# Thresholded attention and a low-rank mixer on one core: new figures and ranks for the planner that orders the kernel, and the last output block on two queues

## The chip, the cores and the metric

The kernel runs on one core of a Trainium2 chip. The metric is the device time of one execution in microseconds; the median of ten executions stands for the kernel. The profile is one further execution, taken apart by the hardware profiler, with its own time. Engines are named as in the profile: PE is TensorE (matmuls; PEld its weight loads), DVE is VectorE, ACT is ScalarE, POOL is GpSimd, SP is SyncE, which here only issues DMAs.

## What is computed

Eight batches, eight heads, 576 rows, head size 64; all inputs and the output are float32.

```python
def _attn_ref(q, k, v, tau):
    scores = scale * np.matmul(q, k.transpose(0, 1, 3, 2))      # scale = 1/8
    thresh = np.max(scores, axis=-1, keepdims=True) - tau
    scores = np.where(scores >= thresh, scores, -1000000000.0)
    scores = scores - np.max(scores, axis=-1, keepdims=True)
    attn = np.exp(scores)
    attn = attn / (np.sum(attn, axis=-1, keepdims=True) + 1e-09)
    return np.matmul(attn, v)

def _moe_ref(x, U, V, w_ch1, w_ch2):          # x: heads side by side, 8 x 576 x 512
    h = x.transpose(0, 2, 1) @ U @ V          # rank 32 over the 576 rows
    u = x + h.transpose(0, 2, 1)
    ch = np.maximum(u @ w_ch1, 0.0) @ w_ch2   # 512 -> 2048 -> 512
    return u + ch
```

So there is attention that keeps only scores within tau of the row's maximum, then a low-rank mix along the rows, then a two-layer mixer along the columns.

## The kernel before, in words

**Attention.** Heads are taken in pairs, 32 pairs (p = 0 to 31), four to a batch. q and k of a pair are loaded by POOL's queue (line 329), turned on PE (383, 396), and copied to SBUF by ACT (389, 402); v is loaded by SP (349) and split into a high and a low bfloat16 part (411, 415). A *score step* is one tile of 128 rows for both heads: 16 float32 matmuls (449). Two pairs share their last half tiles, so two pairs have nine steps and the whole kernel has 144. For each head DVE scales the scores and takes the minimum (462), ACT makes the threshold (475) and the exponential (482), and DVE selects and sums (489). The selected weights are turned by a DMA transpose on SP for both heads at once (502), or, for some tiles of the first pairs, on PE (509) with a copy by ACT (519). A *product* (568 to 591) multiplies one group of turned tiles with v; there are three groups to a pair. For the first four pairs its matmuls are on line 586, later on 582. The sum of the two parts and the division by the row sums (619, 623, 630, or 607 for the first four pairs) write x, of which there are three buffers, batch b using b modulo 3.

**Low rank and mixer.** A pair's columns go through U and V (643, 649, 658), are added (665), narrowed (672), turned on PE (680) and copied (686) into uT. When the four pairs of a batch are through, its mixer can start: 16 `up` tasks of four matmuls each (750) with a ReLU on ACT (740), for odd batches four `rest` tasks (766) for the 64 last rows of two batches together, and then `down`: four blocks of 128 rows, in odd batches a fifth block i = 4 (the last rows of two batches), each block in four quarters of four matmuls (783) into one bank. Each block ends with a sum on DVE (`finish`, 794) and two DMAs on SP (805 and 806, or twice 809). The weights W1 and W2 come in eight loads each by POOL's queue (839, 842), tied to score steps by the lists `W1_AT` and `W2_AT`; `ups` wait for all of W1, `downs` for all of W2. The ReLU outputs of even and of odd batches have one half each of one buffer, so the mixer of a batch starts after that of the batch two before.

**The planner.** The order of instructions on each engine is not written by hand. The class `Order` (66 to 193) takes tasks with an engine, an estimated cost, what they depend on and how many of four PSUM banks they need, runs them through a model of the machine before anything is issued, and emits the instructions in the order that comes out. Each engine then works through its own instructions in that order, and waits on the chip by the buffers that they use. In the model:

- of an engine's tasks that can start within `PATIENCE[engine]` of the earliest, the one of lowest rank is taken; the rank is the time at which it became ready plus an offset from the table `OFF` (three values by name: for the first four pairs, the middle, and the last four pairs);
- `up`, `rest` and `down` have a due step instead (`when`, from `DUE[b]`). Once as many score steps are placed, such a task goes ahead of all others; before, it is taken only if nothing else can start as early;
- a DMA costs its queue `cost`, starts 0.6 later, shares the DMA engines with the other kind of queue (`SHARE`), and is counted as landed `LANDING` later, one value for POOL's queue and one for the others;
- where PE would be idle for longer than 0.45, it is given matmuls on zeros, called fillers (293).

All of `DUE`, `OFF`, `PATIENCE`, `LANDING`, `BOTH` (the cost of issuing one transpose of both heads) and the lists of loads are figures of this planner. What they change is the order in which instructions are issued.

Of the kernel before, what the change touches and what calls it, by code (L numbers as in the profile page):

```python
# [8 lines left out]
P = 128  # L9
# [6 lines left out]
B, H, S, D = 8, 8, 576, 64  # L16
# [4 lines left out]
HB = 64  # L21
# [1 line left out]
NPAIR = H // 2  # L23
NP = B * NPAIR
SOFT = 4
BOTH = 1.9
EARLY = 8


W1_AT = (5, 7, 9, 11, 13, 15, 17, 19)  # L30
W2_AT = (21, 22, 24, 25, 26, 27, 29, 30)

DUE = (30, 48, 99, 104, 159, 168, 132, 156)

# [9 lines left out]
PE, VEC, SCA, POOL, SP = range(5)  # L46
# [19 lines left out]
class Order:  # L66


    SIGNAL = (0.25, 0.18, 0.15, 0.2, 0.1)
    PATIENCE = (0, 0.2, 0.1, 0.55, 0)  # L70


    BEGIN = (1.2, 4.5, 0.7, 1.3, 0.7)
    LANES = 8
    SHARE = (0.8, 0.2)
    LANDING = (2.3, 1.8)
    SWITCH = {"quadrants": 0.145, None: 0.095}
    PARTS = {"S": "quadrants"}


    OFF = {
        "copy_main": (37, 15, -1), "copy_rest": (-1, -8, -1), "copy_tt": (-23, -22, -3),
        "copy_u": (-22, -16, -2), "copy_u4": (0, 21.25, 0), "copy_w": (39.75, -1, -1),
        "down": (0, 0, 0), "exponential": (21, 43, -10.5), "finish": (-2, -4, -1),
        "first": (-300, 0, 0), "high": (3, -26, -32), "inverse": (-19, -21, 31.5),
        "join": (-22, -6, -4.25), "load": (16, 20, 2), "low": (0, 0, 0),
        "low_part": (-22, -19.5, -40), "low_rank": (-20, -28, -3), "make": (10.75, -2, -2),
        "narrow": (-24, 15, -1), "narrow_u": (-21, 20.25, -1), "narrow_u4": (1, 9, 1),
        "norm": (-24, 2, -4), "product": (-21, 6, -2), "relu": (-2, -11, -2), "rest": (0, 0, 0),
        "scores": (-26, -8, -9), "select": (4.75, 49.25, 29.5), "send": (2, 2, 2),  # L90
        "spread": (-23, -7.25, -3), "spread4": (-1, 15, -1), "spread_v": (16, 5, 5),
        "sum_u": (-21.5, -11, -1.5), "sum_u4": (1, 1, 1), "sums": (0, -1, -1),
        "threshold": (-27, -6, -13), "turn4": (-1, -1, -1), "turn_main": (-2, -1, -4),
        "turn_pe": (-25, 13, -1), "turn_rest": (-3, -2, -2), "turn_u": (-23, -6, -3),
        "turn_w": (-20, 0, 0), "up": (0, 0, 0), "values": (20, 20, 20), "weigh": (-23, -4, -8),
        "weights": (3, 5, 5),
    }

    def __init__(self, nbanks, filler):
# [97 lines left out]
def kernel(  # L197
# [12 lines left out]
    nc = tc.nc  # L210
# [87 lines left out]
    done = {}  # L298

    def got(*key):  # L300
        return done.get(key)
# [126 lines left out]
    def score_tasks(p, i):  # L428
# [51 lines left out]
        for x in range(2):  # L480
            def exponential(_, x=x, e_sb=e_ring[tiles[0] % NS], s_sb=s_ring[tiles[0] % NS]):
                nc.scalar.activation(out=e_sb, in_=s_sb, func=ACT.Exp, bias=m[:, x:x + 1],  # L482
                                     scale=-1.0)

            ex = add(SCA, 0.73, exponential, [mins[x], got("w", tiles[0] - NS)])

            def select(_, x=x, w_sb=w_ring[n % (NW // 2)][:, x, :], e_sb=e_ring[tiles[0] % NS],
                       s_sb=s_ring[tiles[0] % NS]):
                nc.vector.scalar_tensor_tensor(  # L489
                    out=w_sb[:, 0:S], in0=s_sb, scalar=thr_[:, x:x + 1], in1=e_sb,  # L490
                    op0=ALU.is_le, op1=ALU.mult, accum_out=pr.den[:, i, x:x + 1])

            sel = done["w", tiles[0]] = add(
                VEC, 0.77, select, [ex, thr, got("wT", tiles[0] - NW), got("rec", p - 4),
                              got("den4", p - 3)])


            both = not (p < EARLY and 1 <= i < 4)

            def turn_w(_, xs=slice(0 if both else x, x + 1)):  # L500
                to = pr.wT[:, xs, :, i * P:(i + 1) * P] if i < 4 else wT4[:, xs, :, HB:HB + P]
                nc.sync.dma_start_transpose(
                    to.rearrange("p x k r -> p (x k) r"),
                    w_ring[n % (NW // 2)][:, xs, :].rearrange("p x c -> p (x c)"))

            def turn_pe(t, w_sb=w_ring[n % (NW // 2)][:, x, :]):
                ps = bank[t.got[0]][:, 0:320].bitcast(BF16)
                for kt in range(NT):
                    nc.tensor.transpose(ps[:, kt * P:(kt + 1) * P],
                                        w_sb[:, kt * P:(kt + 1) * P], identb)  # L510

            free = [got("AV", p - 2, c) for c in range(2)] if i < 4 else \
                [got("AV", a, 2) for a in (p - 2, p - 1)]
            if i < 4 and (x == 1 and p < EARLY and i >= 1 or p == NPAIR - 1 and i == 3):
                t = done["wT", tiles[0]] = add(PE, 0.28, turn_pe, [sel] + free, banks=1,
                                               kind="wT")

                def copy_w(_, x=x, t=t):
                    nc.scalar.copy(
                        out=pr.wT[:, x, :, i * P:(i + 1) * P],  # L520
                        in_=bank[t.got[0]][:, 0:320].bitcast(BF16).rearrange(
                            "p (k r) -> p k r", k=NT))

                t = add(SCA, 0.68, copy_w, [t], frees=[t])
            elif both and not x:
                t = None
                first_sel = sel
            elif both:
                t = done["wT", tiles[0]] = done["wT", tiles[0] - 1] = add(
                    SP, BOTH, turn_w, [first_sel, sel] + free, dma=2.2)  # L530
            else:
                t = done["wT", tiles[0]] = add(SP, 1.28, turn_w, [sel] + free, dma=1.1)
            if t:
                done.setdefault(("wTs", p, i // 2), []).append(t)
                if i == 4:
                    done.setdefault(("wTs", p + 1, 2), []).append(t)
            tiles[0] += 1
            done.setdefault(("den", p), []).append(sel)
# [9 lines left out]
    def value_tasks(p):  # L548
# [16 lines left out]
        for g, tiles_ in enumerate(((0, 1), (2, 3), (4,))):  # L565
            n = len(tiles_)

            def product(t, tiles_=tiles_):
# [19 lines left out]

            av = done["AV", p, g] = add(
                PE, (0.64 if soft else 0.56) * n, product,  # L590
                done["wTs", p, g] + [done["vlo", p], got("AV", p - 1, g)], banks=1, kind="AV")

            def rows(g=g):
                if g < 2:
# [136 lines left out]
    def mixer_tasks(b):  # L731
# [15 lines left out]
        for ft in range(16):  # L747
            def up(t, ft=ft):
                for dt in range(4):
                    nc.tensor.matmul(bank[t.got[0]], W1b[:, dt, ft * P:(ft + 1) * P],  # L750
                                     bt.uT[:, dt, :], start=(dt == 0), stop=(dt == 3))

            t = add(PE, 0.862, up, uT + weights1 + done.get(("o", b - 2), []), banks=1, kind="p1",
                    when=due + 38.75 * ft / 16)
            done["p1", b].append(t)
            lo = 640 * bt.odd
            relus.append(relu_task(t, slice(ft, ft + 1), lo, lo + 512))
        if bt.odd:

            done["p1r", b] = []  # L760
            for g in range(4):
                def rest(t, g=g):
                    for n in range(4):
                        ft = 4 * g + n
                        for dt in range(4):
                            nc.tensor.matmul(bank[t.got[0]][:, n * P:(n + 1) * P],  # L766
                                             W1b[:, dt, ft * P:(ft + 1) * P], bt.uT4[:, dt, :],
                                             start=(dt == 0), stop=(dt == 3))

                t = add(PE, 0.9, rest, [done["uT4", b], got("o4", b - 2)] + weights1, banks=1,  # L770
                        kind="p1", when=due + -11.75 + 9.75 * g)
                done["p1r", b].append(t)
                relus4.append(relu_task(t, slice(4 * g, 4 * g + 4), 512, 640))

        done["o", b] = []
        for i in range(NT if bt.odd else 4):
            halves = []
            for g in range(4):
                def down(t, i=i, g=g, halves=halves):
                    ch = bank[(halves[0] if g else t).got[0]]  # L780
                    lo = 512 if i == 4 else i * P + 640 * bt.odd
                    for ft in range(4 * g, 4 * g + 4):
                        nc.tensor.matmul(ch, R2[:, ft, lo:lo + P], W2b[:, ft, :],  # L783
                                         start=(ft == 0), stop=(ft == 15))

                when = due + 124 if i == 4 and b < B - 1 else due + 20.5 + 0.25 * (i + g / 4) / 4
                halves.append(add(PE, 0.865, down, (relus4 if i == 4 else relus) + weights2 + halves,
                                  banks=int(not g), kind="ch", when=when))

            o = o_ring[done.setdefault("os", 0) % 3]  # L790
            done["os"] += 1
# [11 lines left out]
            def send(_, i=i, o=o):  # L803
# [1 line left out]
                    nc.sync.dma_start(ov[b, :, i, :], o[0:HB, :])  # L805
                    nc.sync.dma_start(ov[b, :, 5 + i, :], o[HB:P, :])
                else:
                    for e in (bt.even, bt):
                        nc.sync.dma_start(ov[e.b, :, 4, :], o[e.h4, :])

            outs.append(add(SP, 1.2, send, [t], dma=0.9, ndma=2))
            outs.pop(0)
# [100 lines left out]
```

## Time and profile before

| what | us |
|---|---|
| median of ten executions | 623.88 |
| lowest and highest of the ten | 623.18, 633.45 |
| the profiled execution | 634.22 |
| its span, first to last instruction | 632.4 |
| PE busy, of it fillers | 607.2, 20.3 |
| DVE busy | 521.6 |
| ACT busy | 479.4 |
| POOL busy | 285.5 |

The profiled execution is one at the upper end of the ten, so its stages can't be read as those of the median without a correction. The busy time of PE is that of matmuls whose ends are modelled and that overlap; gaps between groups are a better sign of loss than its share. The four groups that use most of PE are the score steps (179.1 us), `down` (133.3), `up` (120.0) and the products of line 582 (90.2).

On DVE the select takes 845 ns and the scaling with the minimum 751 ns for one head's tile, each followed by some 82 ns for reading the sum; two heads make a step, so a step occupies DVE for about 3.5 us. A transpose (502) is issued by SP in 1.35 us and lands 4.0 us after its issue in the median; an output block of 64 rows (128 KB) lands after 2.5 us; loads of q and k take 3.9 to 4.7 us, a part of W1 8.8.

### The profile page before, as it was taken

The page shows a single profiled execution, that of the slowest core. Times are in us where ns is not written, and L with a number is a line of the kernel's source. Part 1 is how long each engine was busy: PE and PEld are TensorE (multiplying, and loading weights), DVE is VectorE, ACT ScalarE, POOL GpSimd, SP SyncE. Part 2 cuts the span into 40 slices and gives each one's busy share as a digit, 9 for nine tenths or more (in the row PEclk, how much of TensorE's full clock was granted, in tenths as well). Part 3 has the DMA queues.
Part 4 walks back from the last instruction along what each step waited for, and adds up shares of the span by engine and source line. Part 5 has one row for each costly group of instructions (what it writes and reads, how often), then busy time and mean ns, then how long its engine had stood idle before and what let it go on. Part 6 is the DMA issues. An engine that isn't in the chain of part 4 may idle for free.

```text
span 632.4 us, 16829 instructions
## 1 busy us (share of the span) xinstructions
PE 607.2 (96%) x6286; PEld 355.5 (56%) x6374; DVE 521.6 (82%) x1406; ACT 479.4 (76%) x983; POOL 285.5 (45%) x396
## 2 busy tenths in 40 slices
PE   8979689999999999999999999999999999999996
PEld 3545356566565555555565555555665546555543
DVE  5988599789988899989988999989989898993202
ACT  5767488997888867997788977798787877894440
POOL 8964245745544345546555454445555513121000
PEclk9998799999999999999999999999999999999999
DMA  7999989985887799889997798989997785553303
GB/s 159 161 133 149 125 131 159 173 128 132 170 133 144 116 167 173 156 134 165 156 153 150 130 162 161 154 140 155 153 161 160 147 134 108 110 96 68 67 1 83
DMA packets 205105, 86.27 MB, mean 136 GB/s; under 512 B 183136, under 2 KB 195376, under 8 KB 205024
## 3 DMA queue, kind: packets, MB, share of 16 engines
q1 hardware_dynamic: 190096, 62.23, 61.7%
q0 software_dynamic: 14048, 22.76, 19.6%
q8 instruction: 50, 0.82, 0.6%
q10 hardware_dynamic: 880, 0.21, 0.2%
q14 instruction: 31, 0.25, 0.1%
HBM read 36.86 MB, written 9.44 MB: 73 GB/s over the span
## 4 chain that ended last, share of the span: by engine, by line
PE 84%; DVE 6%; DMA 5%; issue 3%; ACT 1%; SPq 1%; DVEq 0%; ACTq 0%
PE scores L449 23%; PE bank L783 20%; PE bank L750 16%; PE bank L582 12%; DMA wT_ring<-w_ring 4%; PE bank L383 4%; DVE w_ring L489 2%; DVE s_sb L462 2%; PE bank L766 2%; PE bank L643 1%; PE bank L658 1%; PE bank L680 1%; PE bank L396 1%; DMA vraw_ring<-in_v_dram 1%; PE bank L586 1%
## 5 line engine op out<-in xcount | busy, mean ns | idle before, releaser
L489 DVE SCALAR_TENSOR_TENSOR w_ring<-s_sb,thr,e_sb 128x576 bf16<-128x576 f32 x288 | 238.1, 845 | 11.1 <-ACT thr L475 5.1
L462 DVE TENSOR_SCALAR_CACHE_REDUCE s_sb<-scores 128x576 f32<-128x576 f32 x288 | 207.9, 751 | 40.8 <-PE scores L449 37.6
L482 ACT ACTIVATE e_sb<-s_sb,m 128x576 bf16<-128x576 f32 x288 | 217.3, 770 | 30.2 <-DVE s_sb L462 28.9
L449 PE MATMUL scores<-qkT 64*64 64x288 f32 x2304 | 179.1, 419 | 0.8 <-DVE s_sb L462 0.7
L783 PE MATMUL bank<-W2b,R 128*128 128x512 bf16 x541 | 133.3, 380 | 2.4 <-issue 0.6
L630 POOL TENSOR_TENSOR x<-x,rec 128x256 f32<-128x256 f32 (+1 forms) x84 | 58.9, 702 | 169.3 <-DVE x L623 108.2
L750 PE MATMUL bank<-uT,W1b 128*128 128x512 bf16 x470 | 120.0, 380 | 2.5 <-issue 0.5
L449 PEld LDWEIGHTS scores<-qkT 64*64 64x64 f32 x2304 | 78.3, 133 | 73.9 <-issue 19.6
L740 ACT ACTIVATE R<-bank 128x512 bf16<-128x512 f32 x144 | 84.5, 594 | 22.3 <-PE bank L750 14.5
L329 POOL DMA_DIRECT2D qkraw<-in_q_dram x125 | 82.0, 661 | 38.6 <-PE bank L383 32.6
L415 POOL TENSOR_TENSOR vh<-vraw_ring,vh 128x640 bf16<-128x640 f32 x32 | 50.2, 1569 | 78.5 <-ACT vh L411 68.7
L783 PEld LDWEIGHTS <-R 128*128 128x128 bf16 x576 | 53.3, 98 | 56.3 <-issue 5.7
L329 POOL DMA_DIRECT2D qkraw<-in_k_dram x125 | 81.2, 657 | 6.7 <-DMA qkraw<-in_q_dram 3.9
L750 PEld LDWEIGHTS <-W1b 128*128 128x128 bf16 x512 | 46.0, 98 | 52.1 <-issue 10.2
L582 PEld LDWEIGHTS <-wT_ring 128*128 128x128 bf16 x1120 | 64.8, 98 | 12.6 <-issue 8.8
L582 PE MATMUL bank<-vh,wT_ring 128*128 128x128 bf16 x1120 | 71.7, 220 | 0.0
L794 DVE TENSOR_TENSOR o<-bank,x 128x512 f32<-128x512 f32 x36 | 24.4, 682 | 39.7 <-PE bank L783 36.7
L475 ACT ACTIVATE thr<-m,tau_t 128x2 f32<-128x2 f32 x144 | 42.2, 293 | 4.3 <-DVE s_sb L462 3.8
L389 ACT COPY qkT<-bank 128x512 f32<-128x512 f32 x64 | 35.5, 585 | 9.4 <-PE bank L383 9.1
L623 DVE TENSOR_TENSOR x<-bank,x 128x256 f32<-128x256 f32 (+1 forms) x84 | 30.7, 374 | 8.0 <-ACT x L619 7.3
L383 PE MATMUL bank<-ident,qkraw 128*128 128x128 f32 x256 | 35.0, 275 | 2.2 <-DMA qkraw<-in_q_dram 1.5
L619 ACT COPY x<-bank 128x256 f32<-128x256 f32 (+1 forms) x84 | 26.7, 330 | 10.5 <-PE bank L582 9.9
(70 smaller groups left out, 503.1 us busy)
## 6 DMA issues: line engine op xcount, KB each, us to landing
out_dram<-o SPq DMA_DIRECT2D x72, 128.0 KB, 2.5
vraw_ring<-in_v_dram SPq DMA_DIRECT2D x32, 160.0 KB, 3.9
qkraw<-in_k_dram POOLq DMA_DIRECT2D x63, 80.0 KB, 4.7
qkraw<-in_q_dram POOLq DMA_DIRECT2D x62, 80.0 KB, 3.9
vraw_ring<-in_v_dram SPq DMA_DIRECT2D x32, 128.0 KB, 4.2
qkraw<-in_q_dram POOLq DMA_DIRECT2D x63, 64.0 KB, 4.0
qkraw<-in_k_dram POOLq DMA_DIRECT2D x62, 64.0 KB, 4.6
W1b<-in_moe_w_ch_dram POOLq DMA_DIRECT2D x8, 256.0 KB, 8.8
```

The lines of the kernel that those rows point to most:

```text
L329: queue.dma_start(pr.qkraw[part, to, j, :], src[:, j, of, :])
L383: nc.tensor.transpose(bank[t.got[0]][:, i * P:(i + 1) * P], pr.qkraw[:, t0 + i, :, :], ident)
L415: nc.gpsimd.tensor_tensor(out=pr.vh[:, :, :, 1, :], in0=pr.vraw.rearrange("p j t d -> p t j d"), in1=pr.vh[:, :, :, 0, :], op=ALU.subtract)
L449: nc.tensor.matmul(pair_bank[j][part, c, 0:HC], a.tT[hs, 0, rows], a.tT[hs, 1, cs], start=True, stop=True)
L462: nc.vector.tensor_scalar(out=s_sb.rearrange("p (a c) -> p a c", a=2), in0=pair_bank[x][:, :, 0:HC], scalar1=-scale, scalar2=None, op0=ALU ...
L482: nc.scalar.activation(out=e_sb, in_=s_sb, func=ACT.Exp, bias=m[:, x:x + 1], scale=-1.0)
L489: nc.vector.scalar_tensor_tensor(out=w_sb[:, 0:S], in0=s_sb, scalar=thr_[:, x:x + 1], in1=e_sb, op0=ALU.is_le, op1=ALU.mult, accum_out=pr. ...
L582: nc.tensor.matmul(av[:, 2 * a + j, :], w, pr.vh[:, kt, j, :, :], start=first, stop=last_)
L630: nc.gpsimd.tensor_tensor(out=x, in0=x, in1=over_sum(part), op=ALU.mult)
L740: nc.scalar.activation(out=R2[:, fts, lo:hi], in_=bank[t.got[0]].rearrange("p (f c) -> p f c", c=hi - lo), func=ACT.Relu)
L750: nc.tensor.matmul(bank[t.got[0]], W1b[:, dt, ft * P:(ft + 1) * P], bt.uT[:, dt, :], start=(dt == 0), stop=(dt == 3))
L783: nc.tensor.matmul(ch, R2[:, ft, lo:lo + P], W2b[:, ft, :], start=(ft == 0), stop=(ft == 15))
```

## The change

1. `BOTH` goes; a transpose of both heads is counted at 1.4 of issue. `LANDING` becomes (2.0, 1.4) from (2.3, 1.8), `PATIENCE` of POOL and SP rises to 0.9 and 1.35 from 0.55 and 0.
2. `W1_AT`, `W2_AT`, `DUE` and some 30 of the offsets in `OFF` have new values, and the formulas of `when` new constants.
3. A product depends, in the planner, also on `opens`: the tasks after which the buffers of x are free. Before, only the first task that writes x depended on them.
4. The first quarter of a `down` block depends on the first quarter of the block made before it.
5. The block i = 4 sends its two halves for named batches, and for the last batch the second half goes by ACT's queue.

```diff
-W1_AT = (5, 7, 9, 11, 13, 15, 17, 19)
-W2_AT = (21, 22, 24, 25, 26, 27, 29, 30)
-
-DUE = (30, 48, 99, 104, 159, 168, 132, 156)
+W1_AT = (1, 4, 6, 9, 11, 14, 16, 19)
+W2_AT = (20, 21, 23, 24, 25, 26, 28, 29)
+
+DUE = (30, 48, 66, 87, 163, 120, 127, 156)
...
-    PATIENCE = (0, 0.2, 0.1, 0.55, 0)
+    PATIENCE = (0, 0.2, 0.1, 0.9, 1.35)
...
-    LANDING = (2.3, 1.8)
+    LANDING = (2.0, 1.4)
...
-        "copy_main": (37, 15, -1), "copy_rest": (-1, -8, -1), "copy_tt": (-23, -22, -3),
+        "copy_main": (37, 30, -1), "copy_rest": (-1, -8, -1), "copy_tt": (-26, -59, -3),
...
-        "norm": (-24, 2, -4), "product": (-21, 6, -2), "relu": (-2, -11, -2), "rest": (0, 0, 0),
-        "scores": (-26, -8, -9), "select": (4.75, 49.25, 29.5), "send": (2, 2, 2),
+        "norm": (-24, -1, -4), "product": (-21, 20, 8), "relu": (-2, -45, -2), "rest": (0, 0, 0),
+        "scores": (-26, -69.5, -9), "select": (4.75, 49.25, 0.75), "send": (2, 2, 2),
...
-        "threshold": (-27, -6, -13), "turn4": (-1, -1, -1), "turn_main": (-2, -1, -4),
-        "turn_pe": (-25, 13, -1), "turn_rest": (-3, -2, -2), "turn_u": (-23, -6, -3),
+        "threshold": (-27, -6, -29.5), "turn4": (-1, -1, -1), "turn_main": (-2, -37.75, -4),
+        "turn_pe": (-25, 19.75, -1), "turn_rest": (-3, -38, -5), "turn_u": (-50, -6, -3),
...
-                    SP, BOTH, turn_w, [first_sel, sel] + free, dma=2.2)
+                    SP, 1.4, turn_w, [first_sel, sel] + free, dma=2.2)
...
-                done["wTs", p, g] + [done["vlo", p], got("AV", p - 1, g)], banks=1, kind="AV")
+                done["wTs", p, g] + [done["vlo", p], got("AV", p - 1, g)] + opens, banks=1, kind="AV")
...
-                    when=due + 38.75 * ft / 16)
+                    when=due + 35.75 * ft / 16)
...
-                        kind="p1", when=due + -11.75 + 9.75 * g)
+                        kind="p1", when=due + 3.5 + 10.25 * g)
...
-                when = due + 124 if i == 4 and b < B - 1 else due + 20.5 + 0.25 * (i + g / 4) / 4
-                halves.append(add(PE, 0.865, down, (relus4 if i == 4 else relus) + weights2 + halves,
-                                  banks=int(not g), kind="ch", when=when))
+                when = due + 134.5 if i == 4 and b < B - 1 else due + 46.5 + 13.25 * (i + g / 4) / 4
+                halves.append(add(PE, 0.865, down, (relus4 if i == 4 else relus) + weights2 + (
+                    halves or [got("down")]), banks=int(not g), kind="ch", when=when))
+            done["down"] = halves[0]
...
-                    for e in (bt.even, bt):
-                        nc.sync.dma_start(ov[e.b, :, 4, :], o[e.h4, :])
+
+                    nc.sync.dma_start(ov[b - 1, :, 4, :], o[0:HB, :])
+                    last = nc.scalar if b == B - 1 else nc.sync
+                    last.dma_start(ov[b, :, 4, :], o[HB:P, :])
```

More of the change, by code (lines that the diff above doesn't have):

```diff
@@ L25 @@
 SOFT = 4
-BOTH = 1.9
 EARLY = 8
-W1_AT = (5, 7, 9, 11, 13, 15, 17, 19)
-W2_AT = (21, 22, 24, 25, 26, 27, 29, 30)
-DUE = (30, 48, 99, 104, 159, 168, 132, 156)
+W1_AT = (1, 4, 6, 9, 11, 14, 16, 19)
+W2_AT = (20, 21, 23, 24, 25, 26, 28, 29)
+DUE = (30, 48, 66, 87, 163, 120, 127, 156)
 PE, VEC, SCA, POOL, SP = range(5)
@@ L81 @@
     OFF = {
-        "copy_main": (37, 15, -1), "copy_rest": (-1, -8, -1), "copy_tt": (-23, -22, -3),
[L83 to L87, printed above, removed]
@@ L88 @@
-        "narrow": (-24, 15, -1), "narrow_u": (-21, 20.25, -1), "narrow_u4": (1, 9, 1),
-        "norm": (-24, 2, -4), "product": (-21, 6, -2), "relu": (-2, -11, -2), "rest": (0, 0, 0),
-        "scores": (-26, -8, -9), "select": (4.75, 49.25, 29.5), "send": (2, 2, 2),
-        "spread": (-23, -7.25, -3), "spread4": (-1, 15, -1), "spread_v": (16, 5, 5),
-        "sum_u": (-21.5, -11, -1.5), "sum_u4": (1, 1, 1), "sums": (0, -1, -1),
-        "threshold": (-27, -6, -13), "turn4": (-1, -1, -1), "turn_main": (-2, -1, -4),
@@ L94 @@
-        "turn_pe": (-25, 13, -1), "turn_rest": (-3, -2, -2), "turn_u": (-23, -6, -3),
-        "turn_w": (-20, 0, 0), "up": (0, 0, 0), "values": (20, 20, 20), "weigh": (-23, -4, -8),
-        "weights": (3, 5, 5),
+        "copy_main": (37, 30, -1), "copy_rest": (-1, -8, -1), "copy_tt": (-26, -59, -3),
+        "copy_u": (-22, -16, -2), "copy_u4": (0, 21.25, 0), "copy_w": (39.75, -8, -1),
+        "down": (0, 0, 0), "exponential": (21, 43, -29.25), "finish": (-1, 13, -1),
+        "first": (-300, 0, 0), "high": (3, -26, -32), "inverse": (-19, 8.75, 8.5),
@@ new lines @@
+        "join": (-22, -3.25, 2.5), "load": (16, 20, 2), "low": (0, 0, 0),
+        "low_part": (-22, -19.5, -40), "low_rank": (-20, -39, -3), "make": (8.25, -2, -2),
+        "narrow": (-24, 15, -5), "narrow_u": (-21, 20.25, -1), "narrow_u4": (1, 9, 1),
+        "norm": (-24, -1, -4), "product": (-21, 20, 8), "relu": (-2, -45, -2), "rest": (0, 0, 0),
+        "scores": (-26, -69.5, -9), "select": (4.75, 49.25, 0.75), "send": (2, 2, 2),
+        "spread": (-23, -7.25, -3), "spread4": (-1, 21, -1), "spread_v": (1, 5, 5),
@@ L97 @@
+        "sum_u": (-25, -11, 0), "sum_u4": (1, -4, 1), "sums": (-22, -1, -1),
+        "threshold": (-27, -6, -29.5), "turn4": (-1, -1, -1), "turn_main": (-2, -37.75, -4),
+        "turn_pe": (-25, 19.75, -1), "turn_rest": (-3, -38, -5), "turn_u": (-50, -6, -3),
+        "turn_w": (-20, 0, 0), "up": (0, 0, 0), "values": (20, 20, 20), "weigh": (-23, -3, -8),
+        "weights": (-4, 5, 5),
     }
```

## The prediction

> **What bounds the kernel now.** I read the page's slices first, then busy time by stage, then the waits, and at last the order of time at both ends. The slices:
>
> ```profile
> PE   8979689999999999999999999999999999999996
> DVE  5988599789988899989988999989989898993202
> PEclk9998799999999999999999999999999999999999
> ```
>
> TensorE is full from slice 7 (about 100 us) to the last. VectorE is nearly full until slice 36, then almost unused. The loss lies at the start, where TensorE drops to 6 tenths and its clock with it. The stages, cut at the first matmul of a mixer (99.4 us) and behind the last select (573.5 us), with PE, PEld, DVE, ACT and POOL busy in that order:
>
> ```profile
> 0.00:20.00 20.00, 17.05 (x121) 8.29 (x124) 12.33 (x43) 10.79 (x21) 16.97 (x29) 1.00 0.82 148
> 20.00:99.40 79.40, 66.96 (x933) 42.95 (x938) 67.32 (x182) 56.80 (x114) 43.58 (x64) 0.91 1.19 146
> 99.40:573.50 474.10, 469.35 (x4895) 275.82 (x4967) 432.37 (x1168) 394.25 (x819) 223.64 (x302) 1.00 0.83 145
> 573.50:628.00 54.50, 53.87 (x345) 28.43 (x349) 9.14 (x15) 17.54 (x32) 1.29 (x3) 1.00 0.22 48
> ```
>
> In the two later stages TensorE is idle for 4.75 and 0.63 us. In the first 99.4 us it is idle for 99.4 - 84.0 = 15.4 us, and 18.7 us of its busy time are filler matmuls (line 293, 59 of its 64). So 34.1 us of TensorE do nothing there, because no mixer work exists yet and the attention steps run at VectorE's pace. Who stopped TensorE then, and how long transposes took to land (middle answer 30 to 80 us, last one 200 to 300 us):
>
> ```profile
> PE bank L586 <- DMA wT_ring<-w_ring: 7.2, 3, 4.4
> ...
> DMA to landing us min/median/max: 5.0/11.9/15.0
> ...
> DMA to landing us min/median/max: 3.3/3.9/6.9
> ```
>
> The two long ones in order of time:
>
> ```profile
> 45.47 1.25 PE L586 MATMUL bank<-vh,wT_ring 128*128 128x64 bf16 x20 [2.38 <-DMA wT_ring<-w_ring]
> 46.65 2.20 PE L449 MATMUL scores<-qkT 64*64 64x288 f32 x16
> ...
> 70.36 1.25 PE L586 MATMUL bank<-vh,wT_ring 128*128 128x64 bf16 x20 [4.44 <-DMA wT_ring<-w_ring]
> ```
>
> The score step at 39.69 is followed by the next only at 46.65, and that at 63.87 by one at 73.67: 6.96 and 9.80 us, where steps nearby are about 3.3 us apart. That is 3.7 + 6.5 = 10.2 us lost. The profiled execution took 634.22 us (span 632.4 and 1.8 around it), the median of the runs is 623.88: 10.34 less. I conclude that the median run hardly has these two stalls, and carry differences, not absolute times, from the profile to the median. The end:
>
> ```profile
> 613.71 13.98 PE L783 MATMUL bank<-W2b,R 128*128 128x512 bf16 x63
> ...
> 626.24 1.19 SPq L809 DMA_DIRECT2D out_dram<-o  x2
> 627.72 0.69 DVE L794 TENSOR_TENSOR o<-bank,x 128x512 f32<-128x512 f32 x1 [2.11 <-PE bank L783]
> 628.44 0.47 SPq L805 DMA_DIRECT2D out_dram<-o  x1
> 628.96 0.59 SPq L806 DMA_DIRECT2D out_dram<-o  x1
> ```
>
> From the last matmul to the end are 632.4 - 627.7 = 4.7 us: one sum, two issues in a row, one landing.
>
> **What the Trainium skill says.** "DMA: Bandwidth & Descriptors", section "Issuing engines are not separate DMA queues": starting transfers from several engines saves only the sequencer's time of starting them. The trace can show that price (0.47 and 0.59 us an issue), not yet two queues at once here. The same page, "Anatomy of one DMA", puts most of the fixed two microseconds of a transfer on the confirmation of its write; the last outputs land 2.2 to 2.4 us after issue, so that part stays. "TensorE: Matmul & The Clock Gate", Part 1: idleness throttles the array and activity releases it; after the 2.38 us wait a score step took 2.20 instead of 1.20 us, which agrees. "Perfetto Trace Analysis", section "Identifying the Most-Contended Engine", warns that matmul busy time misleads. Here I trust it only since consecutive groups start without gaps: 12 matmuls of line 783 take 2.59 us on the chain, 0.216 each.
>
> **The change part by part.** The program's order is made by a planner; the waits on the chip come from which buffers an instruction uses. Nearly all of the diff therefore moves instructions and adds none.
>
> *The last block by two queues.* Each block's first quarter now follows the previous block's (`got("down")`), so the last block to run is the last made, i = 4 of batch 7, whose second half goes to ScalarE's queue. Now the pair of line 809 takes 1.19 us in a row. ScalarE issued loads in about 0.64 us each at the start and has no work after 614 us, so nothing is queued behind. Gain 1.19 - 0.64 = 0.55 us on the path that sets the end; bounds 0 (both wait elsewhere) and 0.6.
>
> *Chained down blocks.* The 36 sums (line 794) and their matmuls stay; a block that might have run early waits. Cover: other mixer blocks and scores, as TensorE is full. Cost 0; if cover fails, one block of 3.46 us.
>
> *Value products wait for x.* `opens` gates the product instead of only line 619 or 607. In the trace line 619 waits for its product alone (9.9 us in all, 8 times), never for a sum of an old batch; x has three buffers. Cost 0, gain 0. Were it to bind, all of TensorE behind the product would stand.
>
> *Weights earlier.* W1's eight loads go from steps 5 to 19 (every 2) to steps 1 to 19 (every 2.5), W2's from 21 to 30 to 20 to 29. Each is one POOL issue of 0.57 or 0.76 us; none is added. Two W1 loads fall into the first 20 us, where POOL is 16.97 us busy, so up to 1.1 us of q and k issues are pushed back; pair 2's transposes at 22.0 and 26.2 us precede their first use at 35.9 by about 9 us, which hides it. W2 one step sooner can remove the two fillers at 133.7 us: 0.65 us. Thinner W1 traffic should help the transposes between 30 and 80 us.
>
> *New ranks, due steps, patience.* After 99.4 us TensorE does the same work in another order; the most to win is its 4.75 us of idleness, and I count nothing. Batches 2, 3 and 5 come due at steps 66, 87 and 120 instead of 99, 104 and never (there are 144 steps); scores rank higher. More mixer work early means attention ends later. The end allows that only so far: the last select is at 572.6, batch 7's last column copy ends at 590.2, and then 16 ups, 4 rests and 20 quarters need 36 x 0.865 + 4 x 1.06 = 35.4 us, to 625.6; TensorE ends at 627.7, so about 2 us are slack. For the start, the ranks of copies and transposes in the first four pairs go up, and first mixer work may come 2 to 6 us sooner. Only the share of TensorE that did nothing is won: (34.1 - 10.2) / 89 = 0.27, so 0.5 to 1.6 us. I take 1.0; bounds -3 (waits added by a wrong order) to +6 (late transposes exist in the median run too, and go).
>
> *Refitted figures.* A transpose of both heads is counted at 1.4 us of issue and 1.4 of landing instead of 1.9 and 1.8, so products that use it may be placed 0.9 us earlier. Issue measures 1.35 us, so this is truer, but slack shrinks.
>
> Sum: -0.55 - 0.65 - 1.0 = -2.2 us. In the profiled execution's terms 634.2 becomes 632.0; on the median 623.88 becomes 621.7.
>
> **The rivals.**
> *A shorter start (617.9).* Of the late transposes some part, say 4 us, is in every execution, and spread loads remove it: 621.7 - 3.8. For: the median landing of 11.9 us is no single outlier. Against: the two stalls alone account for the whole distance to the median.
> *Only reordering (623.3).* The start is set by VectorE and nothing but the 0.55 us is won. For: VectorE is busy for 67.3 of 79.4 us there, and most of its rest is the stalls. Against: the fillers at 133.7 hang on weights that now come sooner.
> *Waits for transposes (slower, 629).* Products of line 582 reach TensorE before the transposes land. For: slack is cut by 0.9 us, and between 300 and 500 us transposes land in 4.2 us in the median but up to 8.9. Against: no such wait after 99.4 us now. Behind such a product stand the next scores, and so VectorE. If 18 of the 84 products wait 0.4 us each, 7.2 us are added: 621.7 + 7.2 = 628.9. From 2.2 us of waits the gain is gone; from 5.3 it is slower beyond doubt.
>
> **How the numbers follow.** Within 0.5% means 620.8 to 627.0, about what a measurement of this kernel can tell from no change. Forecast 0.34 (its own range 619.5 to 623.0), shorter start 0.24, only reordering 0.20, waits 0.22. Of the forecast 0.14 lies below 620.8; of the waits 0.02 lie inside. Faster: 0.14 + 0.24 = 0.38; same: 0.20 + 0.20 + 0.02 = 0.42; slower 0.20. The range leaves out the outer part of the shorter start (below 616.5) and of the waits (above 629): about one in ten each.
>
> **What would show it.** Right: the last two issues overlap on SP and ACT and end some 0.5 us nearer to the last sum; no fillers between 99 and 570 us; the first matmul of line 750 comes 2 us or more sooner than two stall-free steps would put it (about 89 us); TensorE idle below 5 us in the middle. Wrong: TensorE waiting for transposes in the middle, fillers there, or a gap between the last select and batch 7's ups.

## The result, and the profile after

| | before | after |
|---|---|---|
| median of the runs, us | 623.68 (622.55 to 634.90, 49 runs) | 621.14 (619.87 to 623.33, 14 runs) |
| profiled execution, us | 634.22 | 620.25 |
| its span, us | 632.4 | 618.5 |
| first matmul of a mixer, us | 99.5 | 83.7 |

The ratio of the two is 0.9954, with a 95% interval from 0.9936 to 0.9972: 2.5 us less. The interval leaves out no change, but the gain lies within the 0.5% that the prediction took as the bound. Nine of the 49 runs of before took over 627 us, and none of the 14 of after or of the 62 of e2, e5 and e8 below, so the medians compare the usual runs. The two profiled executions are 14 us apart, 10 of them because the one of before has the two late transposes that the prediction took out. So the kernel before was run with a profile once more, unchanged (e1): 623.07 us, with a span of 621.3. This execution stands for before in all that follows. (The median of before is 623.68 over the 49 runs beside after; the prediction's 623.88 is that of ten.)

The slices of the page of after:

```profile
PE   7989999999999999999999999999999999999997
...
DVE  5999998799988999899997999899998889797101
...
PEclk9999999999999999999999999999999999999999
```

TensorE is full from slice 4 on and its clock is never cut, whereas before it fell to 6 tenths in slice 5, and its clock to 8 and 7 tenths in slices 4 and 5. That is the visible difference of the two pages, and most of it belongs to one execution, not to the change. The stages of after, cut near the first mixer matmul, at 564.2 us and at the start of the last sum (PE, PEld, DVE, ACT and POOL busy, then clock, DMA share and GB/s):

```profile
0.00:83.60 83.60, 75.71 (x1005) 46.17 (x1014) 75.10 (x216) 63.79 (x126) 59.57 (x89) 1.00 1.07 168
83.60:564.20 480.60, 475.68 (x4943) 278.37 (x5016) 435.75 (x1176) 397.75 (x824) 227.62 (x305) 1.00 0.83 144
564.20:614.00 49.80, 49.43 (x331) 26.71 (x335) 9.57 (x17) 18.20 (x34) 1.90 (x4) 1.00 0.28 55
```

and the same of before (e1):

```profile
0.00:88.70 88.70, 81.91 (x1062) 48.93 (x1063) 79.27 (x224) 67.45 (x133) 60.99 (x94) 1.00 1.05 165
88.70:564.20 475.50, 475.50 (x4989) 277.06 (x4987) 431.54 (x1169) 394.67 (x820) 224.28 (x301) 1.00 0.84 145
564.20:616.60 52.40, 52.37 (x331) 27.09 (x328) 8.61 (x14) 17.29 (x31) 1.23 (x2) 1.00 0.20 43
```

The first stage is 5.1 us shorter. Busy time of TensorE can't be trusted for more: in the middle stage after, 4943 matmuls stand beside 5016 weight loads, so some 70 records are missing and the 4.9 us "idle" are no idleness. I therefore count work by weight loads, each times the pitch at which its kind follows itself in stretches without gaps (0.0706 us for a score matmul, 0.216 for one of 512 columns, 0.0557 of 128, 0.0292 for a product of the first pairs, 0.109 for a turn of q or k), fillers as none. What a stretch lasts beyond that sum is TensorE's *lost time*:

| TensorE's lost time, us | to 100 us | 100 to 560 | 560 to the last sum |
|---|---|---|---|
| before (e1) | 34.6 | 13.35 | 1.0 |
| after | 32.2 | 13.4 | 0.8 |

A group that straddles a cut is counted on both sides here. With each load counted once, where it starts, the rows are 35.0, 14.7 and 1.2 for before and 33.0, 14.45 and 0.8 for after, so the parts are good to about half a microsecond: 2.0 to 2.4 us were won before 100 us, at most 0.25 in the middle, 0.1 to 0.4 at the end. Who stopped TensorE longest in after, and in before (e1):

```profile
PE bank L382 <- DMA qkraw<-in_q_dram: 1.8, 1, 1.8
PE bank L292 <- DVE idle L231: 1.2, 1, 1.2
PE bank L679 <- ACT ub L671: 1.2, 1, 1.2
PE bank L782 <- issue: 0.8, 5, 0.2
PE bank L585 <- DMA wT<-w_ring: 0.7, 1, 0.7
```

```profile
PE bank L509 <- DVE w_ring L489: 1.3, 3, 0.6
PE bank L293 <- DVE idle L232: 1.2, 1, 1.2
PE scores L449 <- DVE s_sb L462: 1.1, 2, 0.7
```

In this execution of before no matmul waits for a transpose of selected weights (line 502): the long stalls are not part of its usual run. Its start is slow for another reason: the last steps of pair 3 on the way to the mixer. The cast that opens them starts at 79.70 us and the last copy into uT at 87.99; after, at 77.88 and 83.16. Of the 4.8 us at the copy, 1.8 come from ahead of the cast and 3.0 from the chain itself. Most of that is one place in TensorE's order: the last product with V (line 657, 658 in before) starts 0.04 us behind the end of the cast that it needs (648, 649 in before) in after, and 2.1 us behind it in before, where other work stands ahead of it. Before (e1), then after:

```profile
81.62 0.24 ACT L649 CAST tt<-bank 128x128 bf16<-128x128 f32 x1
...
83.97 0.40 PE L658 MATMUL bank<-tt,Vb 128*128 128x128 bf16 x4
...
87.99 0.61 ACT L686 COPY uT<-bank 128x512 bf16<-128x512 bf16 x1
...
88.75 1.03 PE L750 MATMUL bank<-uT,W1b 128*128 128x512 bf16 x4
```

```profile
79.47 0.25 ACT L648 CAST tt<-bank 128x128 bf16<-128x128 f32 x1
...
79.76 0.38 PE L657 MATMUL bank<-tt,Vb 128*128 128x128 bf16 x4 [0.19 <-ACT tt L648]
...
83.16 0.57 ACT L685 COPY uT<-bank 128x512 bf16<-128x512 bf16 x1
...
83.65 1.03 PE L749 MATMUL bank<-uT,W1b 128*128 128x512 bf16 x4
```

The tail of after, in order of time:

```profile
613.98 0.69 DVE L794 TENSOR_TENSOR o<-bank,x 128x512 f32<-128x512 f32 x1 [2.70 <-PE bank L782]
614.70 0.47 SPq L809 DMA_DIRECT2D out_dram<-o  x1
614.70 0.55 ACTq L811 DMA_DIRECT2D out_dram<-o  x1
```

The two issues overlap. From the start of the sum to the end of the span are 4.50 us, against 4.69 in e1.

### The profile page after: what moved, and what is told of

It reads as the page before. It is cut to its first block, busy times and chain, and to the rows that moved or that the text cites. A ratio compares the mean times of both kernels' runs of the same rounds, so it can differ in the third digit from the quotient of the medians.

```text
span 618.5 us, 16818 instructions
## 1 busy us (share of the span) xinstructions
PE 600.8 (97%) x6276; PEld 351.2 (57%) x6363; DVE 521.1 (84%) x1406; ACT 479.7 (78%) x983; POOL 289.1 (47%) x396
## 4 chain that ended last, share of the span: by engine, by line
PE 84%; DVE 8%; issue 4%; DMA 2%; ACT 1%; SPq 1%; ACTq 0%; DVEq 0%
PE scores L448 22%; PE bank L782 19%; PE bank L749 18%; PE bank L581 13%; DVE w_ring L488 4%; PE bank L382 4%; DVE s_sb L461 3%; PE bank L765 2%; PE bank L642 2%; DMA wT<-w_ring 1%; PE bank L679 1%; PE bank L657 1%; PE bank L395 1%; DMA vraw_ring<-in_v_dram 1%; ACT e_sb L481 1%
## 5 line engine op out<-in xcount | busy, mean ns | idle before, releaser
L782 PE MATMUL bank<-W2b,R 128*128 128x512 bf16 x542 | 131.5, 380 | 2.4 <-issue 0.8
L414 POOL TENSOR_TENSOR vh<-vraw_ring,vh 128x640 bf16<-128x640 f32 x32 | 52.3, 1634 | 89.9 <-ACT vh L410 64.8
```

The lines of the kernel that those rows point to most:

```text
L414: nc.gpsimd.tensor_tensor(out=pr.vh[:, :, :, 1, :], in0=pr.vraw.rearrange("p j t d -> p t j d"), in1=pr.vh[:, :, :, 0, :], op=ALU.subtract)
L782: nc.tensor.matmul(ch, R2[:, ft, lo:lo + P], W2b[:, ft, :], start=(ft == 0), stop=(ft == 15))
```

## The experiments

Two theories stood at the start. *Order*: the new ranks bring the first mixer work sooner, and TensorE loses less there. *Traffic*: the weights, spread out from step 1, no longer delay the transposes. Beside them stood the price of the second queue, and whether the other edits are worth nothing, as the prediction had it.

**e1, before once more.** No edit.

> The kernel before, unchanged, for a profile of an execution near its median. Theory A (the start is set by VectorE and the median has no long wait for a transpose): first mixer matmul at 88 to 91 us, TensorE idle plus fillers ahead of it 23 to 26 us, waits of TensorE for transposes under 2 us in all. Theory B (some 4 us of late transposes are in every execution): waits for transposes 3 us or more, first mixer matmul after 92 us.

623.07 us, first mixer matmul at 88.7 us, no wait for a late transpose. That is the "about 89" which the prediction had worked out for a run without stalls.

**e2, one queue.** Both halves of the last block leave by SP.

```diff
-                    last = nc.scalar if b == B - 1 else nc.sync
+                    last = nc.sync
```

> The changed kernel with both halves of the last block on SP's queue, nothing else. Theory A: 0.2 to 0.55 us more than the changed kernel, so 0.9957 to 0.9963 of the kernel before; from the last sum to the end 4.7 us instead of 4.52. If the two halves share the DMA engines so that the second lands no sooner: the same 0.9954.

622.19 us, 0.9974 (0.9954 to 0.9993). Its tail:

```profile
615.83 0.69 DVE L794 TENSOR_TENSOR o<-bank,x 128x512 f32<-128x512 f32 x1 [2.71 <-PE bank L782]
616.55 0.47 SPq L809 DMA_DIRECT2D out_dram<-o  x1
617.07 0.59 SPq L811 DMA_DIRECT2D out_dram<-o  x1
```

The second issue ends 1.83 us behind the start of the sum, 1.27 with two queues: 0.56 won, as predicted. But from the end of issue to the end of the span are 2.87 us with one queue and 3.23 with two, so 0.37 is given back. The last landing of e1 and that of ScalarE's transfer in after:

```profile
DMA to landing us min/median/max: 2.3/2.3/2.3
```

```profile
DMA to landing us min/median/max: 2.6/2.6/2.6
```

The later transfer takes 0.3 us longer from issue to landing when both leave together. Whether that comes of leaving together or of ScalarE's queue, no run separates. The queue is worth 0.19 us: from the last sum to the end all five profiles with one queue take 4.69 to 4.70 us, all eight with two 4.50 to 4.51. The medians of e2 and after lie 1.05 us apart; the other 0.9 can't be put down to the queue. Every other instruction keeps its place, e2's profile has one wait of 2.2 us for a transpose at 162 to 165 us, a place that the edit doesn't touch, and the two intervals overlap.

**e3, the new middle alone.** Before, with the new `DUE`, `when` formulas and gate, and the middle and end columns of `OFF`; first column, loads, figures, chain and queue as before.

```diff
-        "scores": (-26, -8, -9), "select": (4.75, 49.25, 29.5), "send": (2, 2, 2),
+        "scores": (-26, -69.5, -9), "select": (4.75, 49.25, 0.75), "send": (2, 2, 2),
...
-                    when=due + 38.75 * ft / 16)
+                    when=due + 35.75 * ft / 16)
...
```

> The kernel before with the new due steps, formulas of due times, ranks of the middle and the end, and the gate of the products; loads of weights, ranks of the first four pairs, figures, chain and queue as before. Theory A (the gain is made at the start and by the fillers of the end): TensorE full in the middle either way, 0.998 to 1.001 of the kernel before, first mixer matmul within 1 us of before. Theory C (the gain is made by the order of the middle and the end): 0.995 to 0.9965.

631.29 us, 1.0134 (1.0085 to 1.0183): slower by 8 in the median of six runs, which lie from 628.95 to 638.05. In its profile TensorE loses 21.6 us between 100 and 560 us instead of 13.4, and of these 8 us more than 4 between 500 and 560. There it runs out of work:

```profile
508.96 1.02 PE L750 MATMUL bank<-uT,W1b 128*128 128x512 bf16 x4 [0.99 <-DVE x L665]
523.51 1.02 PE L750 MATMUL bank<-uT,W1b 128*128 128x512 bf16 x4 [0.56 <-ACT uT L686]
```

Mixer work waits there for the sums and copies of its own batch. Attention does not end later for it: the last select starts at 560.4 us, in e1 at 560.7. So the ranks of the middle are not worth nothing on their own.

**e4, the old loads.** After, with the two lists of before.

```diff
-W1_AT = (1, 4, 6, 9, 11, 14, 16, 19)
-W2_AT = (20, 21, 23, 24, 25, 26, 28, 29)
+W1_AT = (5, 7, 9, 11, 13, 15, 17, 19)
+W2_AT = (21, 22, 24, 25, 26, 27, 29, 30)
```

> The changed kernel with the weight loads at the steps of before (5 to 19 and 21 to 30). Theory A: the loads are worth some 0.65 us by W2 one step sooner, and a part of the start: 0.9965 to 0.9985 of the kernel before. Theory B (denser W1 loads make transposes late): 1.0 or more, with waits for transposes of 3 us or more before 80 us. If the loads do not matter: 0.9954.

624.65 us, 1.0011 (0.999 to 1.0033): the whole gain is gone. Transposes of line 501 between 60 and 80 us land in 10.6 us in the median, 5.5 in after, the first mixer matmul is at 86.2, and 13 fillers stand between 60 and 80 us instead of 4. This spoke for traffic. Against it, e1 has the same lists, and its transposes land there in 4.0 us. And the lists also change the planner's order on every engine, so e5 and e6 separate the two.

**e5 and e6, the loads moved and nothing else.** Here every instruction of TensorE, VectorE, ScalarE and SP keeps its place, and POOL's keep their order among themselves; only the 16 weight loads are issued elsewhere on POOL. In e5 (after) they go at the old steps, the first five about one load later than in after (21.3 to 51.1 us instead of 13.9 to 43.2); in e6 (before) at the new ones. Both use the same hook:

```diff
+    def issue_due():
+        while parcels and parcels[0][0] <= placed[0] - 1:
+            parcels.pop(0)[1](None)
...
-                fn(t)
+                issue_due()
+                if to is not weights1 and to is not weights2:
+                    fn(t)
...
```

> The changed kernel with every instruction of TensorE, VectorE, ScalarE and SP in its place; only POOL issues the 16 weight loads at the steps of before, which puts the first five about one load later. Theory D (the loads' traffic itself makes the start shorter or longer): 1.000 to 1.003 of the kernel before, as with the old lists, transposes between 60 and 80 us landing in 9 us or more. Theory E (the load steps count because the planner lays out another order around them): 0.995 to 0.997, TensorE's lost time up to 100 us within 0.7 of the changed kernel's 32.1.

> The kernel before with every instruction of TensorE, VectorE, ScalarE and SP in its place; only POOL issues the 16 weight loads at the new steps. Theory D: 0.995 to 0.997 of the kernel before. Theory E: 0.999 to 1.001, lost time up to 100 us within 0.7 of 34.5.

e5: 620.60 us, 0.9959 (0.9948 to 0.9971), the ratio of after, with the first mixer matmul at 83.3 us. e6: 623.86 us, 0.9999 (0.9966 to 1.0031), that of before. Its profile is of an execution of 629.14 us, in which a product waits 3.5 us for a transpose and the first mixer matmul comes at 93.7, so the lost time that was expected for it can't be read there; e6 rests on its median alone. Traffic falls: loads that come late or soon in an unchanged order do nothing that the medians show. The lists matter through the order that the planner makes of them.

**e7, the old ranks of the start.** After, with the first column of `OFF` from before.

```diff
-        "copy_main": (37, 30, -1), "copy_rest": (-1, -8, -1), "copy_tt": (-26, -59, -3),
+        "copy_main": (37, 30, -1), "copy_rest": (-1, -8, -1), "copy_tt": (-23, -59, -3),
...
-        "turn_u": (-50, -6, -3), "turn_w": (-20, 0, 0), "up": (0, 0, 0), "values": (20, 20, 20),
+        "turn_u": (-23, -6, -3), "turn_w": (-20, 0, 0), "up": (0, 0, 0), "values": (20, 20, 20),
...
```

> The changed kernel with the ranks of the first four pairs of before; its order has 57 fillers instead of 62, three of them at the end. The prediction's term for these ranks (1.0 us): 0.9965 to 0.998 of the kernel before, first mixer matmul 2 us or more after 83.7 us. If loads and figures alone make the start: 0.995 to 0.996.

628.99 us, 1.0077 (1.0059 to 1.0094): 7.9 us above after. The first mixer matmul comes at 86.4. There are no fillers between 60 and 80 us, and in both halves of that stretch the clock is cut:

```profile
60.00:70.00 10.00, 9.85 (x153) 7.13 (x151) 8.72 (x24) 7.73 (x15) 3.86 (x6) 0.83 1.28 155
70.00:80.00 10.00, 8.44 (x139) 5.79 (x131) 9.26 (x26) 7.79 (x17) 4.41 (x5) 0.83 0.94 136
```

```profile
71.07 0.44 PE L508 MATMUL bank<-identb,w_ring 128*128 128x128 bf16 x5 [0.39 <-ACT wT_ring L518]
72.32 0.44 PE L508 MATMUL bank<-identb,w_ring 128*128 128x128 bf16 x5 [0.81 <-ACT wT_ring L518]
73.12 2.44 PE L448 MATMUL scores<-qkT 64*64 64x288 f32 x16 [0.36 <-DVE s_sb L461]
75.50 2.32 PE L585 MATMUL bank<-vh,wT_ring 128*128 128x64 bf16 x40
...
77.93 1.33 PE L585 MATMUL bank<-vh,wT_ring 128*128 128x64 bf16 x40
79.19 1.20 PE L448 MATMUL scores<-qkT 64*64 64x288 f32 x16
```

The score step at 73.12 takes 2.44 us and the product behind it 2.32, where those of the same size 4 us later take 1.20 and 1.33. A theory came of this: missing fillers cost e7 its clock, and the clock its time.

**e8, the old due steps.** After, with `DUE` of before.

```diff
-DUE = (30, 48, 66, 87, 163, 120, 127, 156)
+DUE = (30, 48, 99, 104, 159, 168, 132, 156)
```

> The changed kernel with the due steps of before (99, 104, 159, 168, 132, 156 for batches 2 to 7), which moves mixer tasks in the middle only. The prediction (order in the middle is worth nothing while TensorE is full): 0.9945 to 0.9965. Theory C (the middle's order carries the gain): 0.998 or more.

621.13 us, 0.9962 (0.995 to 0.9975): the same as after. That batches 2 and 3 come due 33 and 17 steps sooner, and batch 5 at all, is worth nothing. It also moves little: in the two traces every engine has the same order up to 372 us.

**e9, e7 with more fillers.** 21 fillers, three ahead of each of seven score steps.

```diff
+            if 11 <= n <= 21 and order.spare:
+                for _ in range(3):
+                    fill(order.spare[0])
```

> The changed kernel with the old ranks of the first four pairs, as in the run before, and 21 more fillers: three each ahead of seven of the score steps 11 to 21, all other instructions of TensorE in their order. Theory F (that run lost its time twice: some 3.8 us by a worse order, as its plan says, and some 3.6 us because TensorE, idle without fillers, fell to half its clock at 60 to 63 and 73 to 79 us): 624.5 to 626.5 us, 1.002 to 1.005 of the kernel before, clock 1.00 in every stretch of 10 us. Theory G (order alone, fillers are only lost time): 628.5 to 631, 1.008 or more.

632.62 us, 1.0135 (1.0083 to 1.0186): 3.6 us more than e7. The clock is back between 60 and 70 us, not between 70 and 80:

```profile
60.00:70.00 10.00, 9.64 (x129) 5.50 (x132) 9.55 (x28) 8.45 (x19) 3.88 (x7) 1.00 1.24 144
70.00:80.00 10.00, 7.38 (x102) 4.06 (x94) 7.95 (x22) 7.98 (x15) 6.88 (x9) 0.83 0.80 152
```

The first mixer matmul comes at 90.8 us. A filler writes a PSUM bank, and one of them waits 1.4 us for the reader of its bank, with the next score step behind it:

```profile
PE bank L293 <- DVE x L610: 1.4, 1, 1.4
```

More fillers, put there by hand, cost more than they gave. That the clock cost e7 its time falls with the runs of e7 itself: two of the twenty had a granted clock of 1.00 over their whole span and took 628.44 and 629.42 us, about the median of all. The theory is also no account of e7's profile, which loses only 2.2 us more than after before 100 us but 5.1 more between 100 and 560.

**e10, the old figures.** After, with `PATIENCE`, `LANDING` and the cost of a transpose as before.

```diff
-    PATIENCE = (0, 0.2, 0.1, 0.9, 1.35)
+    PATIENCE = (0, 0.2, 0.1, 0.55, 0)
...
-    LANDING = (2.0, 1.4)
+    LANDING = (2.3, 1.8)
...
-                    SP, 1.4, turn_w, [first_sel, sel] + free, dma=2.2)
+                    SP, 1.9, turn_w, [first_sel, sel] + free, dma=2.2)
```

> The changed kernel with the figures of before (1.9 for a transpose of both heads, LANDING 2.3 and 1.8, PATIENCE 0.55 and 0); ranks, loads and due steps as changed. Theory H (ranks, loads and figures only fit together, any one put back gives the gain up): 1.000 or more of the kernel before; the planner's own end is 10.7 us later than for the changed kernel, of which its figures overstate a part, so 1.004 to 1.014. If the figures alone made the kernel faster or do not matter: 0.995 to 0.997.

632.74 us, 1.0135 (1.0084 to 1.0187): 11.6 us above after, the largest of all. Its end shows the two waits of e3 again:

```profile
509.25 1.02 PE L749 MATMUL bank<-uT,W1b 128*128 128x512 bf16 x4 [0.99 <-DVE x L664]
523.80 1.02 PE L749 MATMUL bank<-uT,W1b 128*128 128x512 bf16 x4 [0.55 <-ACT uT L685]
```

What e3 and e10 share is the new ranks of the middle beside the old figures. With the new figures, in after, the two waits are gone: the new ranks need the new figures.

**e11, no gate.** After, with the product free to start without the buffer of x.

```diff
-                done["wTs", p, g] + [done["vlo", p], got("AV", p - 1, g)] + opens, banks=1, kind="AV")
+                done["wTs", p, g] + [done["vlo", p], got("AV", p - 1, g)], banks=1, kind="AV")
```

> The changed kernel without the gate of the products (opens only on what writes x). The prediction (cost 0, gain 0): 0.9945 to 0.9965 of the kernel before. Theory H: the order comes out otherwise and the planner's own end is 3.5 us later: 0.999 to 1.003.

626.39 us, 1.0046 (1.0029 to 1.0063): 5.3 us above after. The start is that of after (first mixer matmul at 83.8 us), the loss is in the middle, 19.0 us against 13.4. Up to 296 us every engine has the order of after; 3 us more than in after are lost between 300 and 400 us, 1.6 more between 500 and 560. Two of its waits, at 301.69 and 305.10 us:

```profile
301.69 1.02 PE L782 MATMUL bank<-W2b,R 128*128 128x512 bf16 x4 [0.71 <-DVE x L701]
305.10 0.73 PE L581 MATMUL bank<-vh,wT_ring 128*128 128x128 bf16 x10 [1.44 <-DMA wT_ring<-w_ring]
```

In before the planner, given the gate alone, moves no instruction on any engine; in after its absence moves many.

**All of them together.** "Planner's end" is the latest end in the table that the planner makes before it issues anything. It is a figure of the program, not a time of the chip.

| kernel | first mixer matmul | lost to 100 | lost 100 to 560 | median | planner's end |
|---|---|---|---|---|---|
| before (e1's profile) | 88.7 | 34.6 | 13.35 | 623.7 | 619.6 |
| after | 83.7 | 32.2 | 13.4 | 621.1 | 616.4 |
| e8, old due steps | 83.9 | 32.7 | 13.85 | 621.1 | 616.5 |
| e4, old loads | 86.2 | 34.7 | 16.0 | 624.7 | 621.0 |
| e11, no gate | 83.8 | 32.4 | 19.0 | 626.4 | 619.9 |
| e7, old ranks of the start | 86.4 | 34.4 | 18.5 | 629.0 | 620.2 |
| e3, new middle alone | 90.5 | 36.4 | 21.55 | 631.3 | 626.1 |
| e10, old figures | 88.0 | 34.6 | 22.95 | 632.7 | 627.1 |

Old loads, gate, ranks of the start and figures, each put back alone, cost 3.5 + 5.3 + 7.9 + 11.6 = 28 us; the whole change undone costs 2.5. The parts fit each other, and these four have no worth of their own that could be told apart from the rest. The start of after stands on more than one profile: e2, e5, e8 and e11 have its order there, their first mixer matmul comes at 83.0 to 83.9 us, and with each load counted once they lose 31.9 to 33.0 us before 100. For the usual start of before there is e1 alone. The planner's end lies 3.7 to 5.6 us under the median for six of the eight. For e11 it is 6.5 and for e7 8.8 under it, the two of the eight whose profiles show a late transpose in the middle, which the planner doesn't know of. The cut clock of e7 does not tell them apart: the profiles of e3 and e10 have one too.

## Why the prediction was right, and where it was not

The predicted 621.7 us and the measured 621.14 are 0.6 apart, and the likeliest case, a start that is sooner by order with nothing won in the middle, is the one that came. The sum behind it was -2.2 us; the medians differ by 2.5. That the two are so near is in part luck: the start was set too small by 1.0 to 1.4 us, and the queue and the W2 loads together too large by 1.0. Its terms:

- **The start, -1.0.** The mechanism is right and the term too small: 2.0 to 2.4 us. The prediction let the first mixer work come 2 to 6 us sooner than about 89 us; it came 5.1 sooner (83.65 for 88.75). The 1.0 stands for 3.7 us sooner at a share of 0.27, from (34.1 - 10.2) / 89. By weight loads TensorE loses 34.6 of before's first 100 us, a share of 0.35, because a matmul's record lasts longer than its pitch (0.379 us for one of 512 columns that takes 0.216 in a row) and so covers small gaps. 5.1 x 0.27 = 1.4 and 5.1 x 0.35 = 1.8: shift and share were too small in about equal parts. What is left of 2.0 to 2.4 is no more than the counting can tell. "Perfetto Trace Analysis", section "Identifying the Most-Contended Engine", had been cited for just this warning, and the prediction set it aside for the whole trace on the ground of gapless groups, which hold in the middle and at the end, but not at the start.
- **Two queues, -0.55.** The term is too large: 0.19. The issue was worth 0.56, as worked out. The prediction took the landing as staying; it grew from 2.35 to 2.62 us, and 0.37 in all was given back. "DMA: Bandwidth & Descriptors", section "Issuing engines are not separate DMA queues", says that only the sequencer's time is saved. The traces agree, and show that even this is not all kept.
- **W2 a step sooner, -0.65.** Not won there. The fillers at 133.7 us (three, by weight loads) are those that stand at 122.9 in e1, where no stall precedes them; after has three at 115.4, and the middle loses the same. Fillers there had been named as a sign of being wrong. Three other fillers in before at 601.9 us are gone after, and the end loses 0.1 to 0.4 us less.
- **The gate, 0.** Wrong taken by itself: the reason, "line 619 never waits for x", is about the chip, where the gate adds no wait. It works on the planner, which takes another task where it would have placed a product. Without it after loses 5.3 us.
- **Ranks of the middle, patience, figures, 0.** Right as a sum with the rest: 13.35 and 13.4 us are lost in the middle. The bound of 4.75 us on what could be won there was none: it is the idle time of a row with some 70 records missing. Wrong as a statement on each: alone, the new middle costs 8 us, and the old figures 11.6 (e3, e10). The worry "slack shrinks" did not come true in after, where no product of line 581 waits for a transpose. That more early mixer work makes attention end later is what no run shows: e3 loses most toward 560 us, where mixer work ran dry, and its last select comes no later than in e1.
- **Due steps, 0.** Right (e8).
- **Loads, help for the transposes.** The prediction counted nothing for this. The times of issue are worth nothing (e5, e6).
- **The chain of down blocks, 0.** Right: the planner lays out the same order for after without the chain, on every engine.

Of the rivals, *a shorter start by late transposes* falls with e1 for the usual run: no product of before waits for a transpose there for more than 0.2 us, and the loss at the start is the spacing of steps. The two other profiles of before's order do have such a wait, of 4.4 us and (e6) of 3.5; whether the new order keeps it away was not tested. *Only reordering*, in which VectorE sets the start, falls with the 2.0 to 2.4 us. *Waits for transposes* did not come in after, where the products of line 581 wait for none, but it is close: e2, e7 and e11 have single ones of 2.2, 1.7 and 1.4 us, each in its one profiled execution.

What stays open: why exactly e7 and e11 lose 5 us in the middle. The waits shown make up less than half of it; the rest is spread over many steps. Nor does a run tell which of the three figures of e10 the new ranks need.

## What to carry to other kernels

Where a planner orders the work, its ranks, cost figures and load points are one fit: judge the set by a run, and do not read the worth of a part from undoing it, or from what it does alone. To see whether data or order made a difference, move the transfer and hold every other instruction in its place, as in e5 and e6. Price an earlier start by work counted, weight loads times pitch, not by the busy row, and price a second queue with the landing of both transfers, not with the issue alone.

## What the runs showed of the hardware

- Two transfers of 128 KB started at the same time by SP and ScalarE: 0.56 us less issue, but the later one landed 2.62 us after its issue instead of 2.35, and the whole tail was 0.19 us shorter, the same to 0.02 us in thirteen profiles.
- "TensorE: Matmul & The Clock Gate", Part 1, has idleness throttle the array, and speaks of an idle window of about 3.4 us. In e7 the pauses were shorter: the granted clock fell to 0.50 for 3.4 us at 60.6 and again at 74.3 us, behind stretches of about 3.4 us in which TensorE was busy for 2.35 and 1.95 us and no pause was longer than 1.05 and 0.81 us. The score step behind the second took 2.44 us instead of 1.20. The busy row hides the cut, since it counts the slower instructions in full: over 60 to 70 us it reads 98%. Twenty-one fillers (e9) left one of the two cuts and lost more than they gave.
- Transposes of selected weights between 60 and 80 us landed in 10.6 us in the median in e4, in 5.5 in after and in 4.0 in e1. TensorE waited for transposes 2.6 us in all in e4 and 1.0 in after.
